# Filling TensorE's load waits, and putting the x transposes ahead of the output store, in a fused attention and max-out kernel

## The chip, the cores and the metric

The kernel runs on one NeuronCore of a Trainium2 chip. The metric is device time in microseconds, from the first to the last instruction of the core. TensorE does the matrix products, VectorE (DVE), ScalarE (ACT) and GpSimd (POOL) the elementwise work, and SyncE (SP) issues all transfers between HBM and the on-chip memory (SBUF). Matrix products land in PSUM, which here is divided into two pools of four banks.

## The reference

Inputs are float32: x of 8 batches x 8 heads x 512 x 64, state of 8 x 8 x 32 x 64, W1 and W2 of 512 x 1024, Wo of 1024 x 512.

```python
scores = scale * x @ state^T;   a  = softmax(scores)     # 512 x 32 per batch and head
xread  = a @ state
scores2 = scale * state @ x^T;  a2 = softmax(scores2)    # 32 x 512
sread  = a2 @ x
t = concatenate([xread, sread], axis=2)                  # 544 rows per batch and head
t = t.transpose(0, 2, 1, 3).reshape(8 * 544, 512)        # heads side by side
out = maximum(t @ W1, t @ W2) @ Wo
```

The kernel uses max(h1, h2) = h2 + relu(h1 - h2). So out = relu(t (W1 - W2)) Wo + t (W2 Wo). The product W2 Wo is made once; together with W1 - W2 it is held as one matrix, wcat, of 512 x 1536. For the xread rows, t = a @ state, and the small product state @ wcat is made first (SW); then the first layer is a @ SW.

## The kernel before

Every unit is a small function, and their order in the program is the order on each engine (the schedule is manual; the framework only adds the waits). The parts that matter here:

```python
xio, at, keep, big: pools of 2 buffers;  ps, acc: PSUM pools of 4 banks each

# loads, all from SyncE, in this order
load_w(w2f, moe_w2, 0); load_wo(0); load_states(first); load_x(0)
load_w(w2f, moe_w2, 1); load_wo(1); load_w(w1f, moe_w1, 0); load_w(w1f, moe_w1, 1)
load_x(1); load_states(slice(3, 8)); load_x(2)

def warm_up(n):                     # idle matmuls on zeros
    p = bank()
    for k in range(n):
        nc.tensor.matmul(p, warm[:, 0:128], warm, ...)

def states(bs):                     # transposed states into the block-diagonal sbd
    p = bank(BF16)
    ... transposes into p ...
    for g in range(2):
        copy("V", sbd[...], p[...])
        if bs.start == 0:
            negate("A", sneg[...], p[...])        # -state, for W1 - W2 by two products

def compact_x(b, g):                # x to bf16, half of the heads
    copy("A", st[b]["xc"][:, 4 * g:4 * g + 4], xf_t[b][:, 4 * g:4 * g + 4])
def d_xt(b):                        # x transposed, by DMA
    nc.sync.dma_start_transpose(out=st[b]["xt"], in_=xc)
def u_xt(b, g, eng): ...            # the same by TensorE, for batches 0 and 1

def u_exp(b, g):                    # scores of half the heads, exp on ACT
    p = bank()
    ... 8 matmuls p <- xt, sbd ...
    nc.scalar.activation(out=d["e"][:, g], in_=p, func=ACTF.Exp, scale=scale)
def u_norm(b, g, mul):              # VectorE: sum and reciprocal; mul: a = e * 1/sum
def u_sc(b, g, mul=nc.gpsimd): u_exp(b, g); u_norm(b, g, mul)
def u_sr(b): ...                    # sread: 32 small matmuls, reciprocal and multiply on VectorE
def u_srt(b): ...                   # its transpose; the copy on ACT
def d_at(b):                        # a transposed, by DMA
    nc.sync.dma_start_transpose(out=AT[b], in_=st[b]["a"])
def u_at(b, eng): ...               # the same by TensorE, for batches 0 and 1
def u_sw(b, ch): ...                # state @ wcat, 512 columns; copies on VectorE and ACT

def l1(b, fill, fs): ...            # first layer: 2 matmuls per 128 features, relu on ACT and VectorE by turns
def l2_open(b, c): ...              # output chunk c: 2 matmuls with W2 Wo
def l2_add(b, c, fs): ...           # 1 matmul with Wo per 128 features
def l2_close(b, c):
    copy("A" if c % 2 else "V", ob[:, c, :], OB[b][1 + c])
    if b == B - 1: nc.sync.dma_start(out=dst[:, c:c + 1], in_=ob[:, c:c + 1])
    elif c == NC - 1: nc.sync.dma_start(out=dst, in_=ob)
def l2(b, fill):
    for c in range(NC):
        l2_open(b, c); l2_add(b, c, range(NF)); l2_close(b, c)
        run(*fill.get(NF + c, ()))                # slot 8 + c

def w_cast(o, w, ch): ...           # W1 or W2 to bf16: half on VectorE, half on ACT
def wo_cast(ch): ...                # Wo: 2 slices VectorE, 1 ACT, 1 GpSimd
def w_t(ch, half, eng): ...         # W2 transposed by TensorE
def w_wo(ch, i): ...                # W2 Wo: 4 matmuls per i; after the second half the copy to wcat
```

The loop, and the units of batch n = b + 1 that fill its slots:

```python
def fillers(b):
    slot 8:  u_sc(n, 0); compact_x(n + 1, 0); u_sw(n, 0)
    slot 9:  u_sc(n, 1); compact_x(n + 1, 1); u_sw(n, 1)
    slot 10: u_sw(n, 2); u_sr(n); d_at(n)
    slot 11: u_srt(n); d_xt(n + 1)

for b in range(1, B):
    cast_x(b + 2); load_x(b + 3)    # GpSimd; SyncE
    if b == 1: ... states of batches 3 to 7 in slot 8, w_sub(q) (W1 - W2 on VectorE) in slots 8 to 11
    l1(b, fill); l2(b, fill)
    if b == B - 2: moe_sread()      # both layers for the sread rows
```

Of the kernel before, what the change touches and what calls it, by code (L numbers as in the profile page):

```python
# [15 lines left out]
def kernel(  # L16
# [14 lines left out]
    nc = tc.nc  # L31
    B, H, S, D = x.shape
    _, _, Ns, _ = state.shape
    L = S + Ns
    DM = H * D
    FF = moe_w1.shape[1]
    NC = S // 128
# [22 lines left out]
    def copy(eng, o, i):  # L60
        if eng == "A":
            nc.scalar.copy(o, i)  # L62
        elif eng == "V":
            nc.vector.tensor_copy(o, i)  # L64
        else:
            nc.gpsimd.tensor_copy(o, i)  # L66

    def negate(eng, o, i):
        if eng == "A":
            nc.scalar.activation(out=o, in_=i, func=ACTF.Copy, scale=-1.0)  # L70
        else:
            (nc.vector if eng == "V" else nc.gpsimd).tensor_scalar(o, i, scalar1=-1.0, scalar2=None, op0=ALU.mult)

    def run(*units):
        for u in units:
            u()
# [65 lines left out]
    def states(bs):  # L142
        p = bank(BF16)
        n = bs.stop - bs.start
        for q in range(2 * n):
            nc.tensor.transpose(p[:, q * 128:(q + 1) * 128], s_bf[:, 2 * bs.start + q].rearrange("p u d -> p (u d)"), ident)
        for g in range(2):
            copy("V", sbd[64 * g:64 * g + 64, bs, :, g, :],
                 p[64 * g:64 * g + 64, 0:256 * n].rearrange("p (b h n) -> p b h n", b=n, h=H))
            if bs.start == 0:  # L150
                negate("A", sneg[64 * g:64 * g + 64],
                       p[64 * g:64 * g + 64, 0:256 * n].rearrange("p (b i g n) -> p g b i n", b=n, i=4, g=2)[:, g])


    sread_t = consts.tile([128, 4, B * Ns], BF16)
# [11 lines left out]
    def compact_x(b, g):  # L167
        if g == 0:
            st[b]["xc"] = at.tile([128, H, NC * D], BF16, tag="xc", bufs=1, name="xc")
        copy("A", st[b]["xc"][:, 4 * g:4 * g + 4], xf_t[b][:, 4 * g:4 * g + 4])  # L170


    def d_xt(b):
        nc.sync.dma_start_transpose(out=st[b]["xt"], in_=st[b]["xc"].rearrange("p h w -> p (h w)"))
# [10 lines left out]
    def u_sc(b, g, mul=nc.gpsimd):  # L185
        u_exp(b, g)
        u_norm(b, g, mul)
# [26 lines left out]
    def u_sr(b):  # L214

        d = st[b]
        d["sr"] = at.tile([128, 2, D], BF16, tag="sr", name="sr")
        d["rr"] = at.tile([128, 2], F32, tag="rr", name="rr")
# [3 lines that stand above are left out]
                for i in range(4):  # L222
                    nc.tensor.matmul(p[32 * i:32 * i + 32, g * 65:g * 65 + 65], d["e"][:, g, i, c, :],
                                     d["xp"][:, 2 * i + g, c, 0:65],
                                     start=(c == 0 and g == 0), stop=(c == NC - 1 and g == 1))
        pv = p[:, 0:130].rearrange("p (g u) -> p g u", g=2)
        nc.vector.reciprocal(d["rr"], p[:, 64:130:65])
        nc.vector.tensor_mul(d["sr"], pv[:, :, 0:64], d["rr"].unsqueeze(2).to_broadcast([128, 2, D]))

    def d_at(b):  # L230
        AT[b] = keep.tile([128, 2, NC * 128], BF16, tag="at", name="aT")
        nc.sync.dma_start_transpose(out=AT[b].rearrange("p g (c t) -> p (g c) t", t=128),
                                    in_=st[b]["a"].rearrange("p g c i n -> p (g c i n)"))
# [20 lines left out]
    def u_sw(b, ch, engs="VA"):  # L254
        pg = [bank(), bank()]
        two = b < TWO and ch < 2
        terms = ((sbd, w1b), (sneg, w2b)) if two else ((sbd, wcat),)
        for k, (sv, w) in enumerate(terms):
            for i in range(4):
                for g in range(2):  # L260
                    gs = slice(64 * g, 64 * g + 64)
                    nc.tensor.matmul(pg[g][32 * i:32 * i + 32, :],  # L262
                                     sneg[gs, b, i, :] if k else sbd[gs, b, 2 * i + g, g, :],
                                     w[gs, i, ch * 512:(ch + 1) * 512],
                                     start=(k == 0), stop=(k == len(terms) - 1))
        for g in range(2):
            copy(engs[g], SW[b][:, g, ch * 512:(ch + 1) * 512], pg[g])
# [36 lines left out]
    def l2_close(b, c):  # L304
        ob = OB[b][0]
        dst = out[b * L:b * L + S].rearrange("(p c) n -> p c n", c=NC)
        copy("A" if c % 2 else "V", ob[:, c, :], OB[b][1 + c])
        if b == B - 1:
            nc.sync.dma_start(out=dst[:, c:c + 1], in_=ob[:, c:c + 1])
        elif c == NC - 1:  # L310
            nc.sync.dma_start(out=dst, in_=ob)

    def l2(b, fill):
        for c in range(NC):
            l2_open(b, c)
            l2_add(b, c, range(NF))
            l2_close(b, c)
            run(*fill.get(NF + c, ()))

    def moe_sread():  # L320
        NT = B * Ns
# [22 lines left out]
        cs = slice(q * 256, (q + 1) * 256)  # L344
        nc.vector.tensor_sub(wcat[:, :, cs], w1f[:, :, cs], w2f[:, :, cs])

    def w_cast(o, w, ch):
        cs = slice(ch * 512, (ch + 1) * 512)
        copy("V", o[:, 0:2, cs], w[:, 0:2, cs])
        copy("A", o[:, 2:4, cs], w[:, 2:4, cs])  # L350

    def wo_cast(ch):
        for e, k in (("V", slice(0, 2)), ("A", slice(2, 3)), ("P", slice(3, 4))):
            ks = slice(4 * ch + k.start, 4 * ch + k.stop)
            copy(e, wo[:, ks], wof[:, ks])

    def w_t(ch, half, eng):
# [11 lines left out]
    def w_wo(ch, i):  # L369
        if ch == 0:  # L370
            WO[i] = acc()
        for f in range(4 * ch, 4 * ch + 4):
            nc.tensor.matmul(WO[i], w2t[:, i, f, :], wo[:, f, :], start=(f == 0), stop=(f == NF - 1))  # L373
        if ch:
            copy("A" if i % 2 else "V", wcat[:, i, FF:WC], WO[i])


    def fillers(b):
        fill = {}

        def put(slot, *units):
            fill.setdefault(slot, []).extend(units)

        n = b + 1
        if n < B:
            put(8, lambda: u_sc(n, 0))
            put(9, lambda: u_sc(n, 1))
        if n + 1 < B:
            put(8, lambda: compact_x(n + 1, 0))
            put(9, lambda: compact_x(n + 1, 1))  # L390
        if n < B:
            for ch in range(3):
                put(8 + ch, lambda ch=ch: u_sw(n, ch))
            put(10, lambda: u_sr(n), lambda: d_at(n))
            put(11, lambda: u_srt(n))
        if n + 1 < B:
            put(11, lambda: d_xt(n + 1))
        return fill

    for b in range(B):  # L400
        SW[b] = swt[:, b % 2]
    warm_up(9)
    w_cast(w2b, w2f, 0)
    w_t(0, 0, "V")
    w_t(0, 1, "A")
    wo_cast(0)
    cast_states(first)
    w_wo(0, 0)
    w_wo(0, 1)
    states(first)  # L410
    cast_x(0, (("V", slice(0, 4, 2)), ("A", slice(4, 8, 2)), ("V", slice(1, 4, 2)), ("P", slice(5, 8, 2))))
    w_wo(0, 2)
    w_wo(0, 3)
    u_xt(0, 0, "V")
    u_xt(0, 1, "A")
    u_exp(0, 0)
    u_exp(0, 1)
    w_cast(w2b, w2f, 1)
    u_norm(0, 0, nc.vector)
    u_norm(0, 1, nc.gpsimd)  # L420
    w_t(1, 0, "V")
    w_t(1, 1, "A")
    u_sr(0)
    u_at(0, "V")
    u_srt(0)
    wo_cast(1)
    w_cast(w1b, w1f, 0)
    for i in range(4):
        w_wo(1, i)
    u_sw(0, 0)  # L430
    u_sw(0, 2)
    l1(0, {}, range(0, 4))
    for c in range(NC):
        l2_open(0, c)
    w_cast(w1b, w1f, 1)
    u_sw(0, 1)
    cast_x(1, (("P", slice(0, 4, 2)), ("P", slice(4, 8, 2)), ("V", slice(1, 4, 2)), ("A", slice(5, 8, 2))))
    for c in range(NC):
        l2_add(0, c, range(0, 4))
    u_xt(1, 0, "V")  # L440
    u_xt(1, 1, "A")
    l1(0, {}, range(4, 6))
    u_sc(1, 0, nc.vector)
    l1(0, {}, range(6, 8))
    u_sc(1, 1, nc.gpsimd)
    cast_x(2)
    compact_x(2, 0)
    compact_x(2, 1)
    d_xt(2)
    load_x(3)  # L450
    l2_add(0, 0, range(4, 8))
    l2_close(0, 0)
    u_sw(1, 0)
    l2_add(0, 1, range(4, 8))
    l2_close(0, 1)
    u_sw(1, 1)
    l2_add(0, 2, range(4, 8))
    l2_close(0, 2)
    u_at(1, "V")
    u_sw(1, 2)  # L460
    l2_add(0, 3, range(4, 8))
    l2_close(0, 3)
    u_sr(1)
    u_srt(1)
    for b in range(1, B):
        fill = fillers(b)
        if b + 2 < B:
            cast_x(b + 2)
            if b + 3 < B:
                load_x(b + 3)  # L470
        if b == 1:
            for bs in rest:
                cast_states(bs)
                fill[8].append(lambda bs=bs: states(bs))
            for q in range(4):
                fill[8 + q].append(lambda q=q: w_sub(q))
        l1(b, fill)
        l2(b, fill)
        if b == B - 2:
            moe_sread()  # L480
# [30 lines left out]
```

The softmax here doesn't subtract the row's maximum and nothing guards it: scores larger than these inputs give would overflow.

## Time and profile before

Three runs gave 175.39, 175.55 and 175.57 us.

| Engine | busy us | share of the span |
|---|---|---|
| TensorE matmul | 151.2 | 86% |
| TensorE weight load | 70.0 | 40% |
| VectorE | 90.1 | 51% |
| ScalarE | 78.2 | 45% |
| GpSimd | 32.8 | 19% |

The profile is one execution on the chip. Its parts used below are the timeline (each row a group of instructions of one engine: start, duration, source line, what it writes and reads, and in brackets the idle time before it with what released it), the stage table (per stretch: length, busy time and count of TensorE, its weight loads, VectorE, ScalarE and GpSimd, then the granted TensorE clock, the DMA share and the GB/s), and the DMA issues. A name such as "acc<-wo,w2t" is the output and the operands. Line numbers are those of the kernel in question: L287 is the first layer, L298 and L302 the second, L200 the scores, L262 state @ wcat, L362 the W2 transposes, L373 W2 Wo, L174 and L232 the DMA transposes, L311 the output store.

### The profile page before, as it was taken

The numbers are of one execution on the slowest core, as the hardware profiler recorded it, in microseconds if no ns is written. First come the engines' busy times: TensorE is split into PE (matmuls) and PEld (weight loads), VectorE is DVE, ScalarE is ACT, GpSimd is POOL, SyncE is SP. The second block draws the span as 40 slices with busy tenths as digits, with TensorE's granted clock in tenths as the row PEclk, the third lists the DMA queues.
The fourth block names the chain that finished last, engine by engine and source line by source line (L and its number), as shares of the span: only waits on it lengthen the run. The fifth ranks groups of instructions, "written<-read, shape, count | busy, mean of one in ns | idle before, by whom it ended". The sixth has DMA issues, their size and how long they took to land. (4 is left out here: it accounts for less than half of the span.)

```text
span 175.6 us, 3119 instructions
## 1 busy us (share of the span) xinstructions
PE 151.2 (86%) x1305; PEld 70.0 (40%) x1305; DVE 90.1 (51%) x158; ACT 78.2 (45%) x130; POOL 32.8 (19%) x40
## 2 busy tenths in 40 slices
PE   7378569999689997999879987989798979899991
PEld 2224433345234543444334442434343344654440
DVE  4334871653977599847244642646363547133410
ACT  2413661553856463556427371835373334314111
POOL 2031042000152317024202600260040022000000
PEclk9858955999999999999999999999999999999999
DMA  5999999000099604990797368439305900813133
GB/s 156 351 351 387 388 353 283 5 4 0 0 209 398 233 6 119 279 259 7 207 227 224 59 240 189 172 60 289 73 0 138 269 15 12 241 50 93 26 119 121
DMA packets 34367, 29.04 MB, mean 165 GB/s; under 512 B 21425, under 2 KB 29617, under 8 KB 33457
## 3 DMA queue, kind: packets, MB, share of 16 engines
q1 hardware_dynamic: 34352, 28.84, 55.1%
q8 instruction: 10, 0.16, 0.4%
q14 instruction: 5, 0.03, 0.1%
HBM read 15.20 MB, written 8.91 MB: 137 GB/s over the span
## 5 line engine op out<-in xcount | busy, mean ns | idle before, releaser
L302 PE MATMUL acc<-wo,r 128*128 128x512 bf16 x256 | 60.9, 379 | 1.4 <-DVE r L277 1.4
L302 PEld LDWEIGHTS <-r 128*128 128x128 bf16 x256 | 24.6, 98 | 32.3 <-DVE r L277 1.8
L210 POOL TENSOR_TENSOR a<-e,er 128x512 bf16<-128x512 bf16 x14 | 14.7, 1049 | 94.2 <-DVE er L209 33.4
L287 PE MATMUL ps<-aT,swt 128*128 128x512 bf16 x128 | 29.6, 379 | 3.0 <-ACT ob L62 2.3
L277 DVE TENSOR_SCALAR r<-ps 128x512 bf16<-128x512 f32 x32 | 22.0, 691 | 19.7 <-PE ps L287 19.6
L275 ACT ACTIVATE r<-ps 128x512 bf16<-128x512 f32 x32 | 19.1, 598 | 9.0 <-PE ps L287 9.0
L62 ACT COPY ob<-acc 128x512 f32<-128x512 f32 x16 | 9.4, 586 | 25.3 <-PE acc L302 23.8
L287 PEld LDWEIGHTS <-swt 128*128 128x128 bf16 x128 | 11.9, 98 | 18.1 <-DMA aT<-a 3.9
L207 DVE TENSOR_REDUCE es<-e 128x16 f32<-128x512 bf16 x16 | 11.0, 685 | 15.4 <-ACT e L203 15.4
L64 DVE COPY ob<-acc 128x512 f32<-128x512 f32 x16 | 11.0, 687 | 15.1 <-PE acc L302 15.1
L298 PE MATMUL acc<-swt,aT 128*128 128x512 bf16 x64 | 18.7, 382 | 0.0
L203 ACT ACTIVATE e<-ps 128x512 bf16<-128x512 f32 x16 | 9.6, 600 | 19.4 <-PE ps L200 19.4
L62 ACT CAST swt<-ps 128x512 bf16<-128x512 f32 x24 | 14.0, 590 | 8.5 <-PE ps L262 8.5
L64 DVE CAST swt<-ps 128x512 bf16<-128x512 f32 x24 | 15.7, 658 | 2.8 <-PE ps L262 2.7
L66 POOL CAST xp<-xf 128x2048 bf16<-128x2048 f32 (+1 forms) x9 | 14.1, 1569 | 9.7 <-DMA xf<-in_x_dram 9.7
L373 PE MATMUL acc<-wo,w2t 128*128 128x512 bf16 x32 | 12.1, 552 | 3.4 <-DVE wo L64 3.4
L62 ACT CAST xc<-xf 128x1024 bf16<-128x1024 f32 x12 | 12.4, 1042 | 0.0
L200 PE MATMUL ps<-sbd,xt 128*128 128x64 bf16 x128 | 6.4, 194 | 5.5 <-DMA xt<-xc 4.7
L200 PEld LDWEIGHTS <-xt 128*128 128x128 bf16 x128 | 5.3, 98 | 10.3 <-DMA xt<-xc 7.2
L373 PEld LDWEIGHTS <-w2t 128*128 128x128 bf16 x32 | 4.2, 132 | 10.1 <-issue 9.0
L262 PE MATMUL ps<-wcat,sbd 64*32 64x512 bf16 x144 | 7.7, 386 | 0.0
L298 PEld LDWEIGHTS <-aT 128*128 128x128 bf16 x64 | 4.8, 97 | 6.3 <-issue 2.7
(63 smaller groups left out, 110.0 us busy)
## 6 DMA issues: line engine op xcount, KB each, us to landing
xf<-in_x_dram SPq DMA_DIRECT2D x8, 1024.0 KB, 7.6
out_dram<-ob SPq DMA_DIRECT2D x7, 1024.0 KB, 4.4
w2f<-in_moe_w_dram SPq DMA_DIRECT2D x2, 1024.0 KB, 8.6
wof<-in_moe_w_out_dram SPq DMA_DIRECT2D x2, 1024.0 KB, 9.0
w1f<-in_moe_w_dram SPq DMA_DIRECT2D x2, 1024.0 KB, 13.4
out_dram<-ob SPq DMA_DIRECT2D x4, 256.0 KB, 2.0
out_dram<-obs SPq DMA_DIRECT2D x8, 64.0 KB, 1.7
s_f<-in_state_dram SPq DMA_DIRECT2D x1, 320.0 KB, 16.1
```

Source lines behind the costliest of these rows:

```text
L62: nc.scalar.copy(o, i)
L64: nc.vector.tensor_copy(o, i)
L66: nc.gpsimd.tensor_copy(o, i)
L200: nc.tensor.matmul(p[:, k * 64:k * 64 + 64], d["xt"][:, 4 * i + 2 * g + cp, :], sbd[:, b, 2 * i + g].rearrange("p u n -> p (u n)"), start= ...
L207: nc.vector.tensor_reduce(d["es"][:, g], d["e"][:, g].rearrange("p i c n -> p (i c) n"), axis=mybir.AxisListType.X, op=ALU.add)
L210: mul.tensor_mul(d["a"][:, g].rearrange("p c i n -> p i c n"), d["e"][:, g], d["er"][:, g].rearrange("p (i c) -> p i c", i=4).unsqueeze(3) ...
L275: nc.scalar.activation(out=o, in_=p, func=ACTF.Relu)
L277: nc.vector.tensor_scalar(o, p, scalar1=0.0, scalar2=None, op0=ALU.max)
L287: nc.tensor.matmul(p, SW[b][:, g, f * 128:(f + 1) * 128], AT[b][:, g, :], start=(g == 0), stop=(g == 1))
L298: nc.tensor.matmul(OB[b][1 + c], AT[b][:, g, c * 128:(c + 1) * 128], SW[b][:, g, FF:WC], start=(g == 0), stop=False)
L302: nc.tensor.matmul(OB[b][1 + c], R[b][:, f, c * 128:(c + 1) * 128], wo[:, f, :], start=False, stop=(f == NF - 1))
L373: nc.tensor.matmul(WO[i], w2t[:, i, f, :], wo[:, f, :], start=(f == 0), stop=(f == NF - 1))
```

## The change

It has four parts. Idle matmuls stand in TensorE's waits between the loads. The casts of W2, Wo and W1, and the engines that make them and the copies from PSUM, are put in the order in which the loads land. In the loop both halves of the softmax stand in one slot. The DMA transpose of x is issued ahead of the output store and not after it, with the transpose of the softmax weights right behind it. The halves of W2 and Wo, and the order of the loads except that of x(3), are kept.

```diff
-            if bs.start == 0:
-                negate("A", sneg[...], p[...])
+    def negate_states():
+        for g in range(2):
+            negate("V", sneg[gs], sbd[gs, 0:TWO, g::2, g, :])
 ...
-        elif c == NC - 1:
-            nc.sync.dma_start(out=dst, in_=ob)
+    def l2_out(b):
+        nc.sync.dma_start(out=out[...], in_=OB[b][0])      # after the last slot of l2
 ...
 def fillers(b):
-    slot 8:  u_sc(n, 0); compact_x(n + 1, 0); u_sw(n, 0)
-    slot 9:  u_sc(n, 1); compact_x(n + 1, 1); u_sw(n, 1)
-    slot 10: u_sw(n, 2); u_sr(n); d_at(n)
-    slot 11: u_srt(n); d_xt(n + 1)
+    slot 8:  u_sc(n, 0); u_sc(n, 1); compact_x(n + 1, 0); compact_x(n + 1, 1)
+    slot 9:  u_sw(n, 0)
+    slot 10: u_sw(n, 1); u_sr(n); d_xt(n + 1); d_at(n)
+    slot 11: u_sw(n, 2); u_srt(n)
 ...
-    warm_up(9)
+    warm_up(13)
     w_cast(w2b, w2f, 0)
     w_t(0, 0, "V"); w_t(0, 1, "A")
-    wo_cast(0)
+    warm_up(7)
+    wo_cast(0, (("V", 0, 2), ("A", 2, 3), ("P", 3, 4)))
     cast_states(first)
     w_wo(0, 0); w_wo(0, 1)
     states(first)
+    negate_states()
     cast_x(0, ...)
     w_wo(0, 2); w_wo(0, 3)
+    warm_up(4)
     u_xt(0, 0, "V"); u_xt(0, 1, "A")
     u_exp(0, 0)
+    warm_up(3)
     u_exp(0, 1)
-    w_cast(w2b, w2f, 1)
+    w_cast(w2b, w2f, 1, "VP")
     u_norm(0, 0, nc.vector)
+    u_sr(0)
+    w_t(1, 0, "A"); w_t(1, 1, "A")
     u_norm(0, 1, nc.gpsimd)
-    w_t(1, 0, "V"); w_t(1, 1, "A")
-    u_sr(0)
-    u_at(0, "V"); u_srt(0)
-    wo_cast(1)
+    wo_cast(1, (("V", 0, 3), ("A", 3, 4)))
+    warm_up(8)
+    w_wo(1, 0); w_wo(1, 1)
+    u_at(0, "A"); u_srt(0)
     w_cast(w1b, w1f, 0)
-    for i in range(4): w_wo(1, i)
+    w_wo(1, 2); w_wo(1, 3)
     u_sw(0, 0); u_sw(0, 2)
     l1(0, {}, range(0, 4))
     ... l2_open(0, c) for all c ...
     w_cast(w1b, w1f, 1)
+    cast_x(1, ...)
+    l2_add(0, 0, range(0, 4))
     u_sw(0, 1)
-    cast_x(1, ...)
-    ... l2_add(0, c, range(0, 4)) for all c ...
+    ... l2_add(0, c, range(0, 4)) for the other c ...
     u_xt(1, 0, "V"); u_xt(1, 1, "A")
-    l1(0, {}, range(4, 6))
+    l1(0, {}, range(4, 8))
     u_sc(1, 0, nc.vector)
-    l1(0, {}, range(6, 8))
     u_sc(1, 1, nc.gpsimd)
     cast_x(2)
-    compact_x(2, 0); compact_x(2, 1); d_xt(2)
     load_x(3)
     l2_add(0, 0, range(4, 8)); l2_close(0, 0)
     u_sw(1, 0)
     l2_add(0, 1, range(4, 8)); l2_close(0, 1)
+    compact_x(2, 0); compact_x(2, 1)
     u_sw(1, 1)
+    u_sr(1)
     l2_add(0, 2, range(4, 8)); l2_close(0, 2)
     u_at(1, "V")
-    u_sw(1, 2)
     l2_add(0, 3, range(4, 8)); l2_close(0, 3)
-    u_sr(1)
+    d_xt(2)
+    u_sw(1, 2)
     u_srt(1)
+    l2_out(0)
```

More of the change, by code (lines that the diff above doesn't have):

```diff
@@ L149, in states @@
                  p[64 * g:64 * g + 64, 0:256 * n].rearrange("p (b h n) -> p b h n", b=n, h=H))
-            if bs.start == 0:
-                negate("A", sneg[64 * g:64 * g + 64],
-                       p[64 * g:64 * g + 64, 0:256 * n].rearrange("p (b i g n) -> p g b i n", b=n, i=4, g=2)[:, g])
+    def negate_states():
+        for g in range(2):
+            gs = slice(64 * g, 64 * g + 64)
+            negate("V", sneg[gs], sbd[gs, 0:TWO, g::2, g, :])
     sread_t = consts.tile([128, 4, B * Ns], BF16)
@@ L309, in l2_close @@
             nc.sync.dma_start(out=dst[:, c:c + 1], in_=ob[:, c:c + 1])
-        elif c == NC - 1:
-            nc.sync.dma_start(out=dst, in_=ob)
+    def l2_out(b):
+        nc.sync.dma_start(out=out[b * L:b * L + S].rearrange("(p c) n -> p c n", c=NC), in_=OB[b][0])
     def l2(b, fill):
@@ L318, in l2 @@
             run(*fill.get(NF + c, ()))
+        if b < B - 1:
+            l2_out(b)
     def moe_sread():
@@ L345, in w_sub, with w_cast, wo_cast @@
         nc.vector.tensor_sub(wcat[:, :, cs], w1f[:, :, cs], w2f[:, :, cs])
-    def w_cast(o, w, ch):
+    def w_cast(o, w, ch, engs="VA"):
         cs = slice(ch * 512, (ch + 1) * 512)
[L349 to L354, printed above, removed]
+        for k in range(2):
+            copy(engs[k], o[:, 2 * k:2 * k + 2, cs], w[:, 2 * k:2 * k + 2, cs])
+    def wo_cast(ch, cuts):
+        for e, k0, k1 in cuts:
+            ks = slice(4 * ch + k0, 4 * ch + k1)
             copy(e, wo[:, ks], wof[:, ks])
@@ L374, in w_wo @@
         if ch:
-            copy("A" if i % 2 else "V", wcat[:, i, FF:WC], WO[i])
+            copy("V" if i % 2 else "A", wcat[:, i, FF:WC], WO[i])
     def fillers(b):
@@ L385, in fillers @@
         if n < B:
-            put(8, lambda: u_sc(n, 0))
-            put(9, lambda: u_sc(n, 1))
+            put(8, lambda: u_sc(n, 0), lambda: u_sc(n, 1))
         if n + 1 < B:
-            put(8, lambda: compact_x(n + 1, 0))
-            put(9, lambda: compact_x(n + 1, 1))
+            put(8, lambda: compact_x(n + 1, 0), lambda: compact_x(n + 1, 1))
         if n < B:
[L392 to L395, printed above, removed]
+            put(9, lambda: u_sw(n, 0))
+            put(10, lambda: u_sw(n, 1), lambda: u_sr(n))
         if n + 1 < B:
-            put(11, lambda: d_xt(n + 1))
+            put(10, lambda: d_xt(n + 1))
+        if n < B:
+            put(10, lambda: d_at(n))
+            put(11, lambda: u_sw(n, 2), lambda: u_srt(n))
         return fill
@@ L416 @@
     u_exp(0, 0)
+    warm_up(3)
     u_exp(0, 1)
-    w_cast(w2b, w2f, 1)
+    w_cast(w2b, w2f, 1, "VP")
     u_norm(0, 0, nc.vector)
+    u_sr(0)
+    w_t(1, 0, "A")
+    w_t(1, 1, "A")
     u_norm(0, 1, nc.gpsimd)
-    w_t(1, 0, "V")
-    w_t(1, 1, "A")
-    u_sr(0)
-    u_at(0, "V")
+    wo_cast(1, (("V", 0, 3), ("A", 3, 4)))
+    warm_up(8)
+    w_wo(1, 0)
+    w_wo(1, 1)
+    u_at(0, "A")
     u_srt(0)
-    wo_cast(1)
     w_cast(w1b, w1f, 0)
-    for i in range(4):
-        w_wo(1, i)
+    w_wo(1, 2)
+    w_wo(1, 3)
     u_sw(0, 0)
@@ L435 @@
     w_cast(w1b, w1f, 1)
+    cast_x(1, (("P", slice(0, 4, 2)), ("P", slice(4, 8, 2)), ("V", slice(1, 4, 2)), ("A", slice(5, 8, 2))))
+    l2_add(0, 0, range(0, 4))
     u_sw(0, 1)
-    cast_x(1, (("P", slice(0, 4, 2)), ("P", slice(4, 8, 2)), ("V", slice(1, 4, 2)), ("A", slice(5, 8, 2))))
-    for c in range(NC):
+    for c in range(1, NC):
         l2_add(0, c, range(0, 4))
@@ L441 @@
     u_xt(1, 1, "A")
-    l1(0, {}, range(4, 6))
+    l1(0, {}, range(4, 8))
     u_sc(1, 0, nc.vector)
-    l1(0, {}, range(6, 8))
     u_sc(1, 1, nc.gpsimd)
     cast_x(2)
-    compact_x(2, 0)
-    compact_x(2, 1)
-    d_xt(2)
     load_x(3)
@@ L455 @@
     l2_close(0, 1)
+    compact_x(2, 0)
+    compact_x(2, 1)
     u_sw(1, 1)
+    u_sr(1)
     l2_add(0, 2, range(4, 8))
```

## The prediction

> **What bounds the kernel now.** I read the page's busy slices first: TensorE is busy 86% of the span, so only its idle and slow time (24.4 us idle, more lost to a half clock) can be won. The chain of waits goes no further back than 151 us, so I turned to TensorE's own timeline, where each idle stretch carries its releaser, and then to the SyncE timeline. Two regions carry the loss.
>
> First the prologue, up to about 53 us, from the TensorE timeline (start, duration, instruction group, idle time before it and releaser):
>
> ```profile
> 6.72 1.23 PE L362 MATMUL ps<-ident,w2b 128*128 128x128 bf16 x16 [1.95 <-DVE w2b L64]
> 10.04 3.57 PE L373 MATMUL acc<-wo,w2t 128*128 128x512 bf16 x8 [2.09 <-DVE wo L64]
> ...
> 25.44 6.53 PE L373 MATMUL acc<-wo,w2t 128*128 128x512 bf16 x16 [1.27 <-DVE wo L64]
> 31.90 0.41 PE L262 MATMUL ps<-w1b,sbd 64*32 64x512 bf16 x8
> ...
> 46.53 0.39 PE L302 MATMUL acc<-wo,r 128*128 128x512 bf16 x1 [1.36 <-DVE r L277]
> ```
>
> Sixteen 128x512 matmuls take 6.53 us at 25.44 (0.41 each) where eight take 1.89 us in the loop (0.22 each plus a tail). The stage table says why: the granted clock (its column after the five busy times) is 0.50 from 22 us on.
>
> ```profile
> 22.00:26.30 4.30, 2.86 (x46) 1.67 (x45) 3.10 (x7) 2.74 (x4) 1.78 (x3) 0.50 1.10 354
> 26.30:30.70 4.40, 4.40 (x12) 1.57 (x11) 0.69 (x1) 0.59 (x1) 1.17 (x2) 0.50 1.02 284
> ```
>
> Second, the steady loop. One iteration (one batch's first layer, then four output chunks with the next batch's attention work between them) starts at 85.23 us and the next at 101.56:
>
> ```profile
> 85.23 3.63 PE L287 MATMUL ps<-aT,swt 128*128 128x512 bf16 x16 [0.59 <-ACT ob L62]
> ...
> 92.12 0.41 PE L200 MATMUL ps<-sbd,xt 128*128 128x64 bf16 x8 [1.10 <-DMA xt<-xc]
> ```
>
> The second wait is for the DMA transpose of x. The first is named ACT, but its weight-load twin waits for another thing:
>
> ```profile
> 85.23 0.76 PEld L287 LDWEIGHTS <-swt 128*128 128x128 bf16 x5 [0.92 <-DMA aT<-a]
> ```
>
> so it is the DMA transpose of the softmax weights, aT. The SyncE timeline shows the order that causes both:
>
> ```profile
> 82.12 1.24 SPq L232 DMA_TRANSPOSE aT<-a  x1
> 85.23 0.35 SPq L311 DMA_DIRECT2D out_dram<-ob  x1
> 85.64 4.77 SPq L174 DMA_TRANSPOSE xt<-xc  x1
> 90.46 0.58 SPq L84 DMA_DIRECT2D xf<-in_x_dram  x1
> ```
>
> aT is issued at 82.12 and lands 3.0 us later, when the first layer starts. xt is issued behind the 1 MB output store and lands 6.4 us later at 92.04, just when it is needed or 1.1 us after.
>
> **What the Trainium skill says.** TensorE: Matmul & The Clock Gate, Part 1: the array falls back to half clock after an idle window of about 3.4 us and comes back after as much activity. The trace agrees: 9 us of thin work and gaps (17 to 26 us) is followed by clock 0.50 until about 31 us, and the matmul spacing doubles. DMA: Bandwidth & Descriptors, section Queues, rings and completion order: on each DMA engine descriptors of one queue are consumed in ring order. All transfers here are SyncE's; the trace agrees in that xt moves only after the store in front of it has (DMA busy 86 to 88.7 us with 300 to 390 GB/s, then 88.7 to 91.7 us at about 220 GB/s). SBUF — State Buffer, section Two separate sides: VectorE's two-port operations and GpSimd block each other. The trace shows it: a GpSimd cast of 128x512 takes 0.61 us alone and 1.13 us beside a VectorE cast. This bears on the W2 cast that now goes to GpSimd.
>
> **The change part by part, prologue.** The load order is the same, so I take landing times from before: W2 second half 15.8, Wo second half 18.6, W1 first half 21.3, W1 second half 25.1, x(1) 28.1 us (issue plus time to landing).
> - Idle matmuls: 4 more at the start, then groups of 7, 4, 3 and 8. They sit in waits; warm, 7 cost 1.5 us inside the 2.0 us gap before 10.04, 8 cost 1.7 us. What they buy: the eight matmuls at 10.04 (3.57 us) and the sixteen at 25.44 (6.53 us) at 0.22 each, that is 1.8 and 3.5 us. So 1.8 + 3.0 us.
> - Order: the sneg negation leaves ACT and the VectorE wait on it, so the x(0) casts begin at about 14.0 instead of 15.98, and the x transposes at 14.5 instead of 16.46.
> - The second exp ends at about 18.1 instead of 20.1. Then ACT carries the chain: two w2t copies of 1.0 us (19.4 to 21.3), one Wo slice (to 21.9). Wo times W2 begins at 21.4 instead of 25.44, its fourth matmul at 22.0. Eight matmuls to 23.0, the aT transposes to 23.5, eight matmuls to 25.4.
> - On ACT: wcat 0.6, aT copy 1.0, sread 0.3, W1 cast 1.05, wcat 0.6: W1 ready at 25.9. The state products begin at 25.9 instead of 31.90, and the first layer of batch 0 at 27.4 instead of 33.34. Gain 5.9 us.
> - From there TensorE was nearly full before, so the work moves along. l1 of batch 0 is not split any more, so its last ReLU on VectorE no longer stands behind a reduce and a normalisation; the 1.36 us wait at 46.53 goes. Gain so far 7.2 us.
> - The tail up to the loop is 5.9 us long before (46.9 to 52.8). Now two 1.0 us compactions of x(2) stand on ACT in it, and VectorE has twelve operations of 0.6 to 0.7 us there. I get 6.3 us instead of 5.9. The loop then begins at 46.0 instead of 52.77: gain 6.8 us.
>
> **Loop, with T the start of an iteration.** TensorE's own work is 14.66 us of 16.33 in the stage 85.23 to 101.56; with pipelining 14.45 between starts. The first score matmul stands at T+5.65.
> - Both scores, both exps (0.6 us each) and both compactions (1.04 us each) now stand in one slot: exps end at T+7.2, xc is ready at T+9.1, the second GpSimd multiply (1.05 us) ends at T+10.05.
> - xt is issued at T+9.15, with nothing ahead of it in the queue. Such an issue took 2.04 us before (the first, at 47.06), its data moved from 1.2 to 4.2 us after it. It lands near T+13.5 and is needed at T+20. The 1.1 us wait goes.
> - aT is now issued behind xt: at T+11.35, and its 1.35 us of data come after xt's, T+13.3 to T+14.7, plus about 0.5 us to landing: T+15.2. TensorE would be ready at T+14.45. So aT's wait stays, some 0.7 us, and the period is 15.2 instead of 16.33, 16.55 and 16.36. Three iterations: 1.13 + 1.35 + 1.16 = 3.6 us.
> - Batch 6 has no xt behind it: its xt wait goes (1.1 us), the wait on ACT before the sread layers (0.79) stays, since ACT there has one more copy. 1.1 us.
> - Batch 1: VectorE is busy with hardly a break from 58.6 to 73.4 us (W1 minus W2, states, softmax); the same operations stand there after, so its length stays: 0. Batch 2 wins its small wait and meets the new aT one: 0.2 us.
> - Everything after 151 us is untouched.
>
> Sum: 6.8 + 0 + 0.2 + 3.6 + 1.1 = 11.7 us. The prologue is packed by hand from some forty durations; I take 0.7 us off for waits I did not see: 175.55 − 11.0 = **164.5 us**.
>
> **Rivals.**
> 1. The aT transpose behind xt becomes the bound of the loop. If xt counts 6.3 us from issue to landing also with an empty queue (the first one's recorded value, with a load right behind it), aT lands near T+16.9: four iterations at about 17.0, 0.6 us longer each than before. The gain is then 6.8 + 1.1 − 2.4 = 5.5, time 170 us. Against it: the first one's data had moved by 51.5 us, 4.4 us after issue.
> 2. aT comes early enough: the compactions on ACT end sooner than T+9.1, or two transposes back to back move faster than one by one. Then the loop has no DMA wait left: period 14.5, 4 x 0.7 us more gained, 161.5 us. The 0.7 us is the difference of two sums of ten durations each, so this can't be ruled out; nothing in the profile speaks for it either.
> 3. TensorE falls to half clock in the prologue nonetheless, or ACT (which now has w2t twice, Wo, wcat, aT in a row) is later than I packed it. Then 3 us of the prologue are lost: 167.5 us. The gap between 18.1 and 21.4 is covered by 32 small matmuls, 16 transposes and 8 idle matmuls, which speaks against a cold clock.
> 4. The idle matmuls delay real ones: if operands come early, the eight stand in the way with 1.7 us at most. The Wo cast ends at 21.3 by my count, so this costs 0 to 0.5 us.
> 5. VectorE in batch 1 takes in the prologue's gain. It would if its work were tied to a load; x(3) and the states have landed by then, so no.
>
> **Range and chances.** Between rivals 2 and 3 lies most of what can go wrong by itself: 161 to 168 us, 8 in 10. For less than 2% gain (over 172 us) rivals 1 and 3 would have to come together and worsen: faster 0.94, within 2% 0.04, slower 0.02.
>
> **What would show it.** In the changed profile: clock 1.0 from 14 to 31 us, and the sixteen Wo matmuls in two groups of about 1.9 us each; first layer of batch 0 near 27.4; the first loop iteration near 46.0. In the loop, no wait of the score matmuls for xt; SyncE with xt, aT, store in this order, aT's issue about 2.2 us after xt's; the first layer waiting some 0.7 us for aT; periods near 15.2. I am wrong if the periods stand above 16 (rival 1), if the loop starts after 48 (rival 3), or if batch 1 gets longer than 16.7.

## The result

The changed kernel takes 161.56 us (median of four, 161.46 to 161.77) where the kernel before took 175.52: ratio 0.9207, 95% interval 0.9191 to 0.9223. The prediction was 164.5, with 161 to 168 as its range.

The profiles are set side by side by the starts of the loop iterations (the first row of the first layer, L287 before and L289 after). The first profile of the kernel before had a span of 175.6 us, but it had caught more half clock in the prologue than the typical execution; the "before" column is from a second profile of the same kernel (span 174.5; it is the first experiment below). The time of a run is some 1.8 us more than its span, in both kernels.

| Stage | before, us | after, us | gain | predicted gain |
|---|---|---|---|---|
| start to first loop iteration | 51.66 | 44.48 | 7.2 | 6.8 |
| batch 1 | 16.69 | 15.89 | 0.8 | 0 |
| batch 2 | 15.80 | 15.55 | 0.25 | 0.2 |
| batches 3, 4, 5 | 16.36, 16.49, 16.34 | 14.70, 14.68, 14.74 | 5.1 | 3.6 |
| batch 6, to the sread layers | 16.60 | 15.34 | 1.3 | 1.1 |
| rest | 24.5 | 24.5 | 0 | 0 |

The prologue after, from TensorE's timeline (start, duration, group, idle time and releaser):

```profile
6.73 1.07 PE L367 MATMUL ps<-ident,w2b 128*128 128x128 bf16 x16 [0.48 <-DVE w2b L64]
7.64 1.67 PE L133 MATMUL ps<-warm 128*128 128x512 bf16 x7
9.82 1.89 PE L378 MATMUL acc<-wo,w2t 128*128 128x512 bf16 x8 [0.51 <-DVE wo L64]
...
21.09 1.89 PE L378 MATMUL acc<-wo,w2t 128*128 128x512 bf16 x8
...
23.31 1.89 PE L378 MATMUL acc<-wo,w2t 128*128 128x512 bf16 x8
...
27.03 1.90 PE L289 MATMUL ps<-aT,swt 128*128 128x512 bf16 x7 [0.52 <-DVE swt L64]
```

W2 Wo now runs in groups of eight that take 1.89 us each, where sixteen took 6.53, and it is done by 25.2 us. The first layer of batch 0 starts at 27.03. The same stretches as before in the stage table, where the column after the five busy times is the granted clock, give 1.00 where they gave 0.50:

```profile
22.00:26.30 4.30, 4.20 (x46) 1.96 (x44) 2.00 (x4) 3.19 (x5) 0.11 (x1) 1.00 1.10 347
26.30:30.70 4.40, 3.83 (x20) 1.68 (x18) 3.58 (x6) 3.72 (x6) 1.17 (x2) 1.00 1.05 281
```

The loop, batch 3:

```profile
75.92 3.67 PE L289 MATMUL ps<-aT,swt 128*128 128x512 bf16 x16 [0.18 <-DMA aT<-a]
...
81.58 0.63 PE L202 MATMUL ps<-sbd,xt 128*128 128x64 bf16 x16
...
90.62 3.67 PE L289 MATMUL ps<-aT,swt 128*128 128x512 bf16 x16 [0.17 <-DMA aT<-a]
```

The scores (L202) have no wait any more; the first layer's wait for aT is down from 0.6 us to 0.18. The SyncE timeline has the new order:

```profile
85.06 1.93 SPq L176 DMA_TRANSPOSE xt<-xc  x1
87.09 1.71 SPq L234 DMA_TRANSPOSE aT<-a  x1
90.59 0.36 SPq L314 DMA_DIRECT2D out_dram<-ob  x1
91.00 0.43 SPq L84 DMA_DIRECT2D xf<-in_x_dram  x1
```

With T = 75.92, xt is issued at T+9.14 and lands 4.3 us later; aT is issued at T+11.17 and lands 3.5 us later, at T+14.65.

So the time is close to the prediction, and the stages add up. What follows tests whether the parts did it for the reasons given. In the loop they did, as far as the runs can tell the parts apart. In the prologue they did not quite, and an effect that was not in the prediction at all turned out larger than any part of it.

### The profile page after: what moved, and what is told of

It reads as the page before. It is cut to its first block, busy times and chain, and to the rows that moved or that the text cites. A ratio compares the mean times of both kernels' runs of the same rounds, so it can differ in the third digit from the quotient of the medians.

```text
span 159.9 us, 3154 instructions
## 1 busy us (share of the span) xinstructions
PE 148.1 (93%) x1310; PEld 69.5 (44%) x1331; DVE 90.9 (57%) x158; ACT 77.2 (48%) x129; POOL 32.9 (21%) x40
## 5 line engine op out<-in xcount | busy, mean ns | idle before, releaser
L289 PE MATMUL ps<-aT,swt 128*128 128x512 bf16 x126 | 29.9, 379 | 2.3 <-DMA aT<-a 0.7
L64 DVE CAST swt<-ps 128x512 bf16<-128x512 f32 x24 | 16.3, 686 | 11.2 <-PE ps L264 11.1
L289 PEld LDWEIGHTS <-swt 128*128 128x128 bf16 x128 | 11.9, 97 | 17.4 <-issue 2.9
L300 PE MATMUL acc<-swt,aT 128*128 128x512 bf16 x51 | 15.8, 380 | 1.4 <-issue 1.1
L205 ACT ACTIVATE e<-ps 128x512 bf16<-128x512 f32 x16 | 8.8, 595 | 14.1 <-PE ps L202 13.9
L66 POOL CAST xp<-xf 128x2048 bf16<-128x2048 f32 (+1 forms) x9 | 13.6, 1523 | 8.1 <-DMA xf<-in_x_dram 8.1
L133 PE MATMUL ps<-warm 128*128 128x512 bf16 x33 | 10.2, 451 | 1.4 <-POOL warm L119 1.3
L378 PE MATMUL acc<-wo,w2t 128*128 128x512 bf16 x31 | 7.3, 378 | 0.6 <-DVE wo L64 0.5
L264 PEld LDWEIGHTS <-sbd 64*32 64x32 bf16 x192 | 2.9, 89 | 10.4 <-issue 10.3
L133 PEld LDWEIGHTS <-warm 128*128 128x128 bf16 x35 | 3.7, 112 | 6.0 <-issue 2.6
```

The costliest lines, as they stand in the source:

```text
L133: nc.tensor.matmul(p, warm[:, 0:128], warm, start=(k == 0), stop=(k == n - 1))
L264: nc.tensor.matmul(pg[g][32 * i:32 * i + 32, :], sneg[gs, b, i, :] if k else sbd[gs, b, 2 * i + g, g, :], w[gs, i, ch * 512:(ch + 1) * 512 ...
L289: nc.tensor.matmul(p, SW[b][:, g, f * 128:(f + 1) * 128], AT[b][:, g, :], start=(g == 0), stop=(g == 1))
L300: nc.tensor.matmul(OB[b][1 + c], AT[b][:, g, c * 128:(c + 1) * 128], SW[b][:, g, FF:WC], start=(g == 0), stop=False)
```

## The experiments

In the first runs theory A is the prediction's: three gains that add up, by the clock, by the order of the casts, and by the loop's transfers. In the later ones it is what the text ahead of the run had come to. The rivals are named with each run. The runs were made on several chips, on which the kernel before took 175.5 to 176.5 us, so ratios are to the kernel before on the same chip.

**The kernel before once more.** No edit.

> The kernel before once more, for a second profile of it. The two profiles on hand differ by 15.7 us of span (175.6 and 159.9), the medians by 14.0 (175.52 and 161.56). Theory A: the first profile of before caught more half clock in the prologue than most executions do, so this one has a span near 173.8 us, with the first loop iteration starting near 51 and not at 52.8, and loop periods unchanged at 16.3 to 16.6. Rival: the difference lies in the loop, and the prologue ends at 52.8 again.

Span 174.5, loop from 51.66, periods 16.34 to 16.49 in batches 3 to 5. The first profile's extra 1.1 us lay in the prologue, as theory A had it, if not the 1.8 us that it asked for: the two profiled executions of this kernel are somewhat unlike each other there. The table above uses this profile.

**Only the idle matmuls taken out.**

```diff
-    warm_up(13)
+    warm_up(9)
-    warm_up(7)     # and the 4, the 3 and the 8
```

> The changed kernel with 9 idle matmuls at the start, as before, and none later. Theory A (the clock is worth several us by itself): W2 Wo is computed at half clock again, about 0.2 us more for each of up to 24 matmuls; 165 us (163.5 to 167), clock 0.5 somewhere between 8 and 27 us. Rival B (the new order of the casts makes the prologue's gain, the idle matmuls only fill time): within 0.5 us of the changed kernel, 161.6.

Median 163.97 us, ratio 0.9272 (0.921 to 0.9333), against 0.9207 with them: 0.65% or 1.1 us. The two intervals just overlap, but the profile has a difference of this size too. Theory A's 4.8 us for the clock is wrong, and so is the rival's zero. The profile shows where the 1 us is and where the other 3.7 us are not (the stage table; its clock column again after the five busy times):

```profile
8.00:12.00 4.00, 2.23 (x6) 0.94 (x7) 1.43 (x2) 1.32 (x2) 1.72 (x2) 0.62 1.13 337
20.00:24.00 4.00, 2.08 (x15) 1.08 (x13) 1.96 (x5) 2.76 (x4) 1.73 (x2) 1.00 1.06 376
```

In the stretch of the first eight matmuls of W2 Wo the mean clock is 0.62, and the loop starts 1.0 us later (45.47). The sixteen of the second half, at 22 us, run at full clock with no idle matmul between the loads. So with the new order the clock stays up there by itself.

**Only the group of eight taken out.**

```diff
-    warm_up(8)
```

> The changed kernel without the group of 8 idle matmuls ahead of the second half of W2 Wo. Theory A (that group keeps the clock up for the sixteen matmuls after it): they run at half clock, 3.5 us more, 165 us. Rival (the clock would have held over a gap of 2 us; the group is idle time that costs nothing): 161.5.

161.62 us, ratio 0.9178 (0.9136 to 0.922): the same as the changed kernel. TensorE's timeline:

```profile
21.03 1.89 PE L378 MATMUL acc<-wo,w2t 128*128 128x512 bf16 x8 [1.81 <-DVE wo L64]
```

After 1.81 us of idling the matmuls still take 1.89 us for eight. The rival is right: this group is worth nothing.

**The softmax back in two slots, x transpose still ahead of the store.** The slots 8 to 10 of the kernel before, but with `d_xt(n + 1)` ahead of `d_at(n)` in slot 10, and the store last.

> The changed kernel with the softmax halves and compactions back in two slots (state products too), but the x transpose still ahead of the output store and the softmax transpose behind it. Theory A (both loop parts are needed): the second compaction ends near T+10.7, aT is issued near T+12.7 and lands near T+16.2, so the first layer waits for aT some 1.7 us and the period is about 16.2: 167.5 us. Rival (putting xt ahead of the store is all the loop's gain): 161.6.

168.73 us, ratio 0.9579 (0.9541 to 0.9617). Theory A, by its number (167.5):

```profile
78.37 3.63 PE L289 MATMUL ps<-aT,swt 128*128 128x512 bf16 x16 [1.75 <-DMA aT<-a]
94.60 3.63 PE L289 MATMUL ps<-aT,swt 128*128 128x512 bf16 x16 [1.74 <-DMA aT<-a]
```

The period is 16.23 us and the wait for aT 1.75, where 16.2 and 1.7 were expected. If the softmax is not early, putting xt first moves the wait from xt to aT, and the period stays what it was in the kernel before.

**The softmax in one slot, but store and then xt, as before.**

```diff
             copy of the last chunk
+            l2_out(b)                  # ahead of slot 11
 ...
-    slot 10: d_xt(n + 1); d_at(n)
+    slot 10: d_at(n)        slot 11: ...; d_xt(n + 1)
```

> The changed kernel with the softmax in one slot, but the store issued ahead of the last slot and the x transpose behind it, as before. Theory A: no wait for aT (issued at T+10, landed by T+13.5), but the scores wait 1.1 us for xt in each of five iterations, period about 15.6: 166 us. Rival (the early softmax is all the loop's gain): 161.6.

175.6 us, ratio 1.0 (0.9972 to 1.0028). Neither: not the rival's 161.6, and 9.6 us more than theory A allowed. The wait is on xt, as expected, but it is not 1.1 us:

```profile
85.22 1.04 PE L202 MATMUL ps<-sbd,xt 128*128 128x64 bf16 x16 [2.53 <-DMA xt<-xc]
```

and two of the periods of the profiled execution (177.04 us) are 19.1 us, with a clock of 0.91 in them. In the kernel before, the same order of the same three transfers gave a wait of 1.1 to 1.3 us. Something else had made xt late here. What the early softmax is worth alone, with xt no later than before, is therefore not measured by this run, nor by another.

**The new prologue with the old loop.** `fillers` and the store of the kernel before, in the changed kernel.

> The new prologue with the old loop: softmax in two slots, store issued after the last chunk's copy, x transpose behind it. Theory A (parts add up): the loop periods go back to about 16.3, so 6.5 us more than the changed kernel, 168 us, and the prologue keeps 7.5 us of gain. Rival: the loop takes in part of the prologue's gain or gives part of its own by starting earlier: outside 167 to 169.

179.29 us, ratio 1.0196 (1.0126 to 1.0267): slower than the kernel before. All of the prologue's gain is gone and more. SyncE and TensorE in batch 3:

```profile
77.38 0.35 SPq L314 DMA_DIRECT2D out_dram<-ob  x1
77.79 4.81 SPq L176 DMA_TRANSPOSE xt<-xc  x1
82.65 0.57 SPq L84 DMA_DIRECT2D xf<-in_x_dram  x1
```

```profile
77.37 3.63 PE L289 MATMUL ps<-aT,swt 128*128 128x512 bf16 x16 [0.58 <-ACT ob L62]
...
85.82 0.41 PE L202 MATMUL ps<-sbd,xt 128*128 128x64 bf16 x8 [2.66 <-DMA xt<-xc]
```

Relative to the start of the iteration each transfer is issued within 0.05 us of where it was before (store +0.01, xt +0.42, load +5.28), but xt lands 8.0 us after its issue and not 6.4.

**The kernel before with the idle matmuls.** `warm_up(13)`, and 7, 4, 3 and 8 more in the corresponding waits; nothing else.

> The kernel before with the same idle matmuls (13 at the start, then 7, 4, 3 and 8 in the corresponding waits), nothing else changed. Theory A: clock 1.0 throughout the prologue, W2 Wo at 0.22 us a matmul; 172 us (170.5 to 173). Rival B: no change, 175.5.

182.69 us, ratio 1.036 (1.029 to 1.0429). Both theories are wrong on the time. The clock is 1.0 through the prologue and the loop starts at 47.80 and not at 51.66, so the aim was met, with 3.9 us; but xt lands 7.9 to 8.1 us after its issue, and the scores wait 2.6 to 3.0 us for it. The idle matmuls alone, at the other end of the program, had made the loop slower.

What the three slow kernels have in common is 26 more matmuls, each with a weight load, ahead of the loop: 52 rows of TensorE's program. The Trainium skill (Runtime: NRT & Kernel Launch, Instruction fetch mechanics) says that the program of an engine is fetched in blocks of 16 KiB, 256 instructions, by DMA as the engine uses it up, and that this is mostly hidden. The trace has such transfers: a DMA queue called "instruction", with a packet of 0.02 MB about once per iteration. An iteration is 129 or 130 matmuls and as many weight loads, which is nearly one block, so the packet comes at nearly the same point of every iteration. In the kernel before it came 10.1 us after the start of the iteration of batch 3 (95.3 for the one at 85.23), and 8.1 to 10.0 us after that of the others, when xt had landed. In the new prologue with the old loop it came at +6.3 (83.7), and in the kernel with idle matmuls alone too (86.5 for 80.26). That is when the last packets of xt are under way. The DMA queues of the old loop behind the new prologue, in the 0.1 us from 83.6 (kind, packets, MB, share of 16 engines):

```profile
q8 instruction: 1, 0.02, 60.4%
q1 hardware_dynamic: 33, 0.01, 33.8%
```

60% of 16 engines for 0.1 us is 1.0 us: the record of this one packet lasts from 83.69 to 84.66. The packets of xt, one by one, show what it does. The last of its data has moved by 83.72, 5.9 us after the issue, exactly as early as in the kernel before. Behind the data come packets of 4 bytes, by their place the marks of completion. All but the last two of these have gone by 83.72 as well; the last two go at 84.64 and 84.65, as the instruction packet ends, and xt lands at 85.77. So xt's data are on time, and its last marks are 0.9 us late. The other 0.6 us lie between the last mark and the landing (1.1 us, 0.5 in the kernel before), and their cause stays open.

The four kernels with 26 matmuls more and the store ahead of xt (the next run is the fourth) show the same in all of their 16 late landings, 7.9 to 8.1 us after the issue: the last two marks go within 0.02 us of the packet's end. In batch 2 of each of the four the packet begins 0.006 to 0.12 us after the last mark, and there xt lands on time, after 6.4 to 6.5 us.

Two runs test this against the rival that an early prologue or a warm clock makes xt late.

**The kernel before with 52 more rows.** 26 matmuls of 32x16, in the first wait for W2.

```diff
     def warm_up(n, tiny=0):
         ...
+        for k in range(tiny):
+            nc.tensor.matmul(p[0:32, 0:16], warm[:, 0:32], warm[:, 0:16], ...)
-    warm_up(9)
+    warm_up(9, 26)
```

> The kernel before with 26 tiny idle matmuls (32x16) in the first wait for W2, where TensorE is idle anyway; they add the same 52 rows to TensorE's program as the change's idle matmuls, and nothing else changes. The new prologue with the old loop, and the old kernel with the idle matmuls, both had xt landing 7.9 us after its issue and not 6.4, and in both one 16 KB instruction fetch for TensorE's program ran beside xt's last packets. Theory A (the added rows move the fetch in the loop onto xt): waits for xt of 2.6 to 3 us in the loop and not 1.1, 181 us (179 to 183). Rival B (an earlier prologue or a warm clock is what makes xt late): no change, 175 to 176.5.

186.3 us, ratio 1.0611 (1.0536 to 1.0687). The prologue is what it was (the loop starts at 51.75), its clock still falls, and the loop waits:

```profile
84.27 3.63 PE L289 MATMUL ps<-aT,swt 128*128 128x512 bf16 x16 [0.58 <-ACT ob L62]
92.76 0.41 PE L202 MATMUL ps<-sbd,xt 128*128 128x64 bf16 x8 [2.70 <-DMA xt<-xc]
```

The instruction packet is at 90.7, which is +6.4, and xt lands 8.0 us after its issue. The DMA view of 8 us from the start of this iteration has, in the last place of its line for xt, the time to landing:

```profile
q8 instruction: 1, 0.02, 0.7%
xt<-xc SPq DMA_TRANSPOSE x1, 8.0
```

In the kernel before, the same view from 85.23 has no instruction packet, and

```profile
xt<-xc SPq DMA_TRANSPOSE x1, 6.4
```

So 26 tiny matmuls cost 10.5 us, some eighty microseconds later: the fetch, which the skill calls mostly hidden, is not hidden here. That is 5 us more than theory A's number. Its stage table (iterations of batches 3 and 4) shows where they went:

```profile
84.27:102.20 17.93, 14.66 (x129) 6.55 (x129) 8.08 (x15) 8.24 (x15) 4.05 (x4) 1.00 0.58 162
102.20:121.80 19.60, 16.34 (x130) 7.12 (x130) 8.08 (x15) 8.14 (x14) 4.05 (x4) 0.91 0.53 148
```

A wait of 2.7 us makes an iteration of 17.9 us, 1.6 more than in the kernel before. In batch 4, and again in batch 6, the clock falls as well, to a mean of 0.91 and 0.90; in batch 4 that costs 1.7 us more.

**The new order with the old loop and no added idle matmuls**, so as many rows ahead of the loop as before.

> The new order of the prologue with the old loop and only the 9 idle matmuls of before, so TensorE's program has as many rows ahead of the loop as before. Theory A (row count and fetch): xt lands 6.4 us after its issue, waits of 1.1 us, 170 us (168.5 to 171.5). Rival B (early prologue makes xt late): waits of 2.7 us as in the old loop behind the new prologue, 181 us.

171.92 us, ratio 0.9756 (0.9702 to 0.981); 0.4 us above theory A's range, and 7.4 us faster than with the idle matmuls. The loop starts at 45.62, early, and xt lands 6.4 us after its issue:

```profile
85.54 0.41 PE L202 MATMUL ps<-sbd,xt 128*128 128x64 bf16 x8 [1.13 <-DMA xt<-xc]
```

The instruction packet is at 88.7, +10.0. Both runs go theory A's way: neither the early prologue nor the clock makes xt late. The row count does, by the place of the packet.

**The old prologue with the new loop.** The prologue's order of the kernel before (the state negation on VectorE), `fillers` and store of the changed kernel.

> The old order of the prologue (state negation on VectorE apart) with the new loop, no added idle matmuls. Theory A: the loop's gain stands alone: no wait for xt, periods of 14.7, 6 to 7 us less than before: 169 us. Rival: without the faster prologue the new loop meets another wait: above 171.

167.51 us, ratio 0.9514 (0.9456 to 0.9572): 8.3 us less than before, somewhat more than the 6 to 7 expected. No wait for xt, periods of 14.7:

```profile
97.02 3.66 PE L289 MATMUL ps<-aT,swt 128*128 128x512 bf16 x16 [0.18 <-DMA aT<-a]
111.74 3.64 PE L289 MATMUL ps<-aT,swt 128*128 128x512 bf16 x16 [0.20 <-DMA aT<-a]
```

With this the parts can be put in one table (ratios to the kernel before):

| Prologue | old loop | new loop |
|---|---|---|
| old order | 1 | 0.951 |
| old order, idle matmuls | 1.036 | not run |
| new order | 0.976 | 0.927 |
| new order, idle matmuls | 1.020 | 0.921 |

Without the idle matmuls the two parts add up: 0.049 for the loop behind either prologue. The idle matmuls gain 0.006 with the new loop and lose 0.044 with the old one. In the changed kernel no instruction packet falls on the marks of xt; besides, xt lands some 7 us ahead of its use, so that 1.5 us more would be covered. In the old loop it lands at the last moment, behind a 1 MB store.

**aT ahead of xt.** In slot 10 of the changed kernel `d_at(n)` and `d_xt(n + 1)` change places.

> The changed kernel with aT issued ahead of xt in the same slot. Theory A (the 0.15 to 0.19 us wait at the head of each first layer is aT's landing behind xt): the wait goes, periods 14.5 and not 14.7, 0.7 us less: 160.9 us. Rival (TensorE's own work or a PSUM bank stands behind that wait): no change, 161.5.

161.69 us, ratio 0.9182 (0.9152 to 0.9211): no change, the rival's result. The wait for aT is gone, but one of the same size stands two matmuls later:

```profile
75.59 0.59 PE L289 MATMUL ps<-aT,swt 128*128 128x512 bf16 x2
76.41 3.18 PE L289 MATMUL ps<-aT,swt 128*128 128x512 bf16 x14 [0.23 <-ACT swt L62]
```

TensorE waits there for ACT's copy of the state product (swt) out of a PSUM bank, and ACT has just copied an output chunk. The aT wait hid this one.

**A version that is faster than both.** That led to the last run: aT first, and the transpose of sread, with its copy on ACT, moved into the middle of the last chunk.

```diff
         l2_open(b, c); l2_add(b, c, range(0, 4))
+        if c == NC - 1: u_srt(b + 1)
         l2_add(b, c, range(4, NF)); l2_close(b, c)
-    slot 11: u_sw(n, 2); u_srt(n)
+    slot 11: u_sw(n, 2)
```

> The changed kernel with aT issued ahead of xt, and the transpose of sread with its copy on ACT moved into the middle of the last output chunk, ahead of the state product. Theory A (the wait of 0.8 us ahead of the sread layers and the 0.2 us waits of the first layers both stand behind ACT's copies at the end of the last slot): both go, 160.2 us. Rival (they are only moved): 161.6.

159.56 us (159.31 to 159.67), ratio 0.9068 (0.9031 to 0.9104). In the stage table TensorE's busy time fills the iterations of batches 2 to 5:

```profile
75.89:90.22 14.33, 14.33 (x138) 6.40 (x130) 8.23 (x15) 8.16 (x15) 4.01 (x4) 1.00 0.75 203
90.22:104.54 14.32, 14.32 (x137) 6.39 (x130) 8.23 (x15) 8.15 (x15) 4.00 (x4) 1.00 0.76 202
```

The sread transpose lies one bank and half a chunk ahead of the state product, so the copies on ACT no longer stand in line at the end of the slot; the 0.8 us wait ahead of the sread layers is gone too. Batch 1 pays for it: it takes 17.17 us and not 15.89, since there TensorE waits for sread's multiply on VectorE:

```profile
60.20 0.23 PE L249 MATMUL ps<-ident,sr 128*128 128x128 bf16 x1 [1.13 <-DVE sr L230]
```

A version that keeps the transpose in its old place in that batch alone was not run.

## Why the prediction held, and where it did not

- **Which waits bound the kernel: right.** Half clock and waits for casts in the prologue, xt and aT in the loop. The last 24.5 us were untouched. Why the clock fell is less clear than I wrote. The prediction has 9 us of thin work, 17 to 26 us, followed by half clock, in agreement with an idle window of 3.4 us. But its own stage table has 0.50 from 22 us on, and from 17 us to there no wait of TensorE is longer than 1.2 us. So the trace shows half clock after some 5 us of thin work, without an idle window of that length.
- **Prologue, 6.8 us: 7.2.** The starts came out near (first layer of batch 0 at 27.03 for 27.4, loop at 44.48 for 46.0; the 7.2 us are against the second profile of the kernel before). But the share of the idle matmuls, 1.8 + 3.0 us, was mis-sized: with the new order they are worth 1.1 us, by the run without them. In the old order they are worth 3.9 us of the prologue, by the run with them alone (loop at 47.80 for 51.66), and the new order without them brings the loop forward by 6.2 us (to 45.47). The two win largely the same time; I had given 4.8 of the 6.8 us to the idle matmuls.
- **Rival 4 and the group of eight.** The group costs nothing, as I said, and it gains nothing, which I had not said.
- **xt issued at T+9.15 and landing near T+13.5: right** (T+9.14, T+13.4).
- **aT landing at T+15.2, wait 0.7 us, period 15.2: mis-sized.** It lands at T+14.65, waits 0.18 us, period 14.7. I added the data times of two transfers that stood alone, 2.9 us and 1.35. The 2.9 is that of the first xt in the kernel before, with an instruction packet at its end; the first xt of the changed kernel, without one, moves its data in 2.6. And two in a row move without a gap, where each alone has a slow start and end. The DMA engines from 85 to 91 us in the changed kernel, in 40 slices (busy tenths, GB/s):

```profile
DMA  0000000049999999999999999999999993000000
GB/s 0 0 0 0 0 0 0 0 96 220 210 217 212 205 208 225 220 217 218 217 218 217 176 186 207 236 222 218 210 208 213 213 193 62 0 0 0 0 0 0
```

  Both go through in 26 slices of 0.15 us, 3.9 us, at some 215 GB/s. That is rival 2, for which I had seen nothing to speak. It makes 1.5 us of the 2.9 by which the time came out lower; my sum missed it, and only the range, drawn so as to include that rival, has it.
- **Batch 1, gain 0: 0.8.** VectorE bounds this iteration, as I had it. But its operations do not take the same time: before, one subtraction W1 − W2 stood beside a GpSimd multiply and cast and took 1.63 us and not 1.22. With both multiplies in slot 8, ahead of the subtractions, the slowest takes 1.31. I had seen this blocking between the two engines and applied it only to the cast of W2. But that is 0.4 us. Another 0.6 us is order: one copy of a state product (swt) no longer stands ahead of sread's multiply on VectorE. Against both, the first reduce starts 0.6 us later in the iteration. The rest is not explained.
- **Batches 2 and 6: right** (0.25 for 0.2, 1.3 for 1.1).
- **Rival 1 did not come, and the question behind it was not the right one.** The one landing time of 6.3 us in an empty queue, from which I made it, had an instruction packet beside its tail (at 51.2 us, with the transfer issued at 47.06). That landing shows the same marks that go late, at the packet's end. In the changed kernel all landings of xt are 4.3 to 4.4 us.
- **The parts do not add up in general.** I took the prologue's gain to be carried through the loop. It is with the new loop; with the old one, the same prologue makes the kernel 2% slower than before. I had written that all transfers are SyncE's, and so left out the fetch of TensorE's own program. That the prediction held all the same is luck in this respect: the two parts stood in one change, and the new loop is the one that the fetch does not hurt.

## What to carry to other kernels

A transfer that lands just in time is a hazard, even when it costs only a microsecond in the profile: here a shift in the number of instructions at the other end of the program made it cost nearly three, and part of the clock in some iterations. Issue it as early as its data allow, and ahead of bulk stores. Before filling waits with idle matmuls, close the waits by order; then take the fillers out again one group at a time and keep only those that pay.

## What the runs showed of the hardware

- The fetch of TensorE's program shares the DMA engines with the kernel's own transfers. A 16 KB packet came about once per iteration of some 259 matmuls and weight loads and took about 1.0 us. When it fell on the last completion marks of a 512 KB DMA transpose, these went only at its end, and the transpose landed after 7.9 to 8.1 us and not after 6.4; the data had moved on time. A packet that began 0.006 us behind the last mark did no harm. 52 rows of program, those of 26 tiny matmuls, decided between the two (175.85 and 186.3 us).
- The clock outlasted idle waits of 1.8 and 1.9 us (the second half of W2 Wo at full rate after them). After waits of 2.5 to 3.0 us in the loop it fell in some iterations and not in others, and where it fell the iteration took 1.0 to 1.7 us more.
- Two DMA transposes issued one behind the other, 512 and 256 KB, moved in 3.9 us without a gap, at some 215 GB/s.
